# Fused banded attention and two-layer MLP: first loads cut by partitions, two ScalarE copies moved, score blocks ahead of the merged values placed closer together

## The chip, the cores and the metric

One core of one Trainium2 chip. The time is the device time of one launch in microseconds (us); less is better. Engines are called PE (TensorE), DVE (VectorE), ACT (ScalarE), POOL (GpSimd) and SP (SyncE, which here only issues transfers).

## The reference

```python
# q, k, v: (8, 8, 576, 64) fp32; w_in (512, 2048), w_out (2048, 512)
scores = (q @ k.T) / 8
rel = pos[:, None] - pos[None, :]
heads 0-3: keep 0 <= rel < 32             # a band
heads 4-7: keep 0 <= rel < 128, rel % 4 == 0   # a dilated band
attn = softmax(where(keep, scores, -1e9))
x = (attn @ v).transpose(0, 2, 1, 3).reshape(4608, 512)
h = x @ w_in
g = where(h >= 1, h, where(h <= -1, 0, (h + 1)**2 / 4))
out = g @ w_out
```

## The kernel before

**Attention.** Each of the 64 heads is cut into 6 tiles of 96 queries by 128 keys, which hold the whole band. The dilated heads are rearranged on the host so that they have a band too. For each tile: scores (PE), mask and row minimum of the negated scores (DVE, `masked` L360, `lowest` L288), exp with the row sum (ACT, L386), the sum guarded against zero (`guarded`), its inverse (DVE, L418), a product (`normalised`, L423, POOL or DVE), a transpose (on PE for the first 16 heads, `transpose_pe` L470, with the copy out of PSUM `kept` L476; by DVE later, `turned` L434), and the product with v on PE (`weighted` L540, later `values` L628).

**MLP.** 9 blocks of 512 tokens by 16 slices of the 2048 hidden values make 144 steps. One step is 12 matmuls of 512 columns in `layer1` (L670, into a PSUM bank h0 or h1 by the step's parity), the activation, and 12 matmuls in `layer2` two steps later (L726, into acc0 to acc3). Products are made exact enough by splitting fp32 in a high and a low part, three matmuls for each product. The activation of a step is a chain over two engines: `clamped` y (DVE, L680), `squared` (ACT, L683), `activated` (DVE, L686), `g_high` gh (ACT, L693), `g_low` gl (DVE, L697). The last of them is the last reader of the step's PSUM bank.

**Order of the work.** The first 16 heads and the first 18 steps follow a list of tokens written out by hand (`OPENING`), which orders all five engines. In it a letter is an operation and the number a head or step: q, k, Q, K load; S scores, r `lowest`, e exp, T `transpose_pe`, p `kept`, V `weighted`, A `layer1`, B `layer2`, y s j g d the activation chain, and W n are n matmuls on constants that only keep PE busy (`spin` L273). a, b, j, h, l before wi or wo convert the weights, which arrive as 64-bit words; on ACT these are L202, L208 and L220.

From step 18 on, only PE and SP have a written order: `place(u, op)` puts work at a quarter of a half step (three 512-column matmuls). The scheduler puts ACT, DVE and POOL in an order of its own at build time, after what PE's order makes possible. Heads 16 to 63 come in pairs. For one head, `score_block` makes two tiles' scores (L336) at each of three places, and behind the third `after` starts the split of the next head's q and k (ACT `q_high` L242 and `k_high` L245, DVE `q_low` L249, POOL `k_low` L253), loads and `softmax`. Where a pair's first head is a multiple of 4 (from head 20: 11 pairs, called "around" in the code), the three places of its first head stand at 0, 0.75 and 1.5.

Right behind the third of them `values` is called in the middle of an odd step's `layer1`: the products with v of four heads, in three PSUM tiles. The second tile takes the bank h0 of the step before, so its matmuls wait for that step's gl:

```python
plan = (
    ("att", 2, ((n, 0, 5),)),
    (f"h{(s + 1) % 2}", 1, ((n + 2, 4, 6),)),
    ("att", 2, ((n + 2, 0, 4), (n, 5, 6))),
)
```

At six of the 11 places the bank is that of step 6 of a token block (h_6), at five that of step 14 (h_14).

In the opening, q and k of heads 0 and 1 come as one tile of 128 partitions (head 0 on partitions 0 to 63, head 1 on 64 to 127). `load_q` and `load_k` (L146, L162) fetch the columns of the first three query tiles of both heads, `rest_k` and `rest_q` (L136, L133) the other columns. Copies of the transposed probabilities of heads 10 and 11 (tokens p10.1, p11.1) stand on ACT near step 4, between conversions of weights.

Of the kernel before, what the change touches and what calls it, by code (L numbers as in the profile page):

```python
# [30 lines left out]
B, H, S, D = 8, 8, 576, 64  # L31
DM, DF = 512, 2048
WIN, DIL = 32, 4
QT, NQ = 96, 6
KPAD = S + 32
# [7 lines left out]


OPENING = """
q0 k0 msk K0 Q0 q2 k2 q4 mk2 S0.0 S1.0 S0.1 S1.1 k4 S0.2 S1.2 r0.0 wi0 r0.1 e0.0 r0.2 r1.2 e0.1 r1.0 S0.3 r1.1
e0.2 S1.3 S0.4 S1.4 S0.5 e1.1 S1.5 r0.3 e1.2 k8 r0.4 r0.5 e0.3 k6 r1.5 S2.0 S3.0 r1.3 e0.5 S2.1 wi1 r1.4 S3.1
S2.2 e0.4 S3.2 S2.3 q6 S3.3 e1.3 S2.4 r2.0 S3.4 S2.5 i0 S3.5 v0 r2.1 e1.0 R0 r2.5 e1.5 wo0 n0 r2.2 r2.4 e1.4
wo1 r2.3 r3.3 r3.1 v6 r3.0 awi0 r3.2 z2 W6 T0.0 r3.4 e3.3 r3.5 v4 S4.0 i1 S5.0 p0.0 S4.1 e3.4 S5.1 S4.2 S5.2
e3.5 S4.3 R1 S5.3 T0.1 n1 r4.3 e3.0 r4.0 e2 r4.1 r4.2 r5.3 r5.1 e3.2 r5.0 u2 e3.1 W6 S6.0 bwi0 S7.0 S6.1 S7.1  # L50
i3 S6.2 r5.2 S7.2 e4.3 S6.3 R3 S7.3 i2 jwi0 S6.4 e4.2 n3 S7.4 S6.5 S7.5 e4.0 r6.3 r6.0 e4.1 r6.1 e6.3 r6.2
r7.3 W3 S4.4 e6.1 r7.2 r7.1 e6.2 hwi0 r7.0 R2 e6.0 r6.4 S5.4 S4.5 r6.5 S5.5 e6.4 r7.5 T3.0 wi9 r7.4 e6.5 r4.5
# [12 lines left out]
p8.1 hwi4 T9.0 g2 T9.1 B1.0 p9.0 wi15 lwi4 e11 q12 V8.0 p9.1 d2 jwo2 wi12 e10.3 V8.1 e10.2 u11 e10.5 hwo2 B1.1  # L65
wo7 bwi5 y3 i10 B1.2 i11 jwi5 wo14 x8.0.0 lwo2 s3 B1.3 R10 R11 hwi5 j3 A4.0 q14 x8.1.0 x8.1.1 n11 g3 A4.1 n10
wo12 awo3 A4.2 l8.0.0 awi6 A4.3 l8.1.0 bwo3 wo13 l8.1.1 B2.0 d3 bwi6 lwi5 jwo3 B2.1 B2.2 awo4 T11.0 y4 hwo3
T10.0 B2.3 jwi6 p11.0 lwo3 p10.0 s4 A5.0 bwo4 A5.1 j4 hwi6 awi7 T10.1 jwo4 A5.2 g4 p10.1 lwi6 bwi7 A5.3 d4
hwo4 T11.1 V10.0 y5 p11.1 V10.1 jwi7 lwo4 x10.0.0 s5 B3.0 l10.0.0 x10.1.0 j5 x10.1.1 B3.1 hwi7 l10.1.0 awo5
B3.2 lwi7 l10.1.1 awi8 B3.3 bwo5 S12.0 S13.0 g5 S12.1 jwo5 S13.1 S12.2 S13.2 bwi8 S12.3 S13.3 A6.0 d5 hwo5  # L70
r12.0 awo6 r12.1 A6.1 lwo5 r12.2 r12.3 e12.0 r13.3 A6.2 r13.0 bwo6 r13.1 r13.2 A6.3 e13.3 jwi8 e13.2 B4.0 jwo6
hwi8 e13.1 e13.0 y6 S12.4 S13.4 e12.3 S12.5 S13.5 B4.1 r12.4 e12.2 k16 r13.5 s6 r13.4 hwo6 v12 r12.5 B4.2
# [24 lines left out]
def body(ctx, tc, q, k, q2, k2, v, v1, fixed_in, w_in, w_out, out):  # L97
    nc = tc.nc
# [7 lines left out]
    msk = fixed[:QT, : 3 * 128].rearrange("p (k j) -> p k j", k=3)  # L106
# [18 lines left out]
    def borrow(name):  # L125
        return pool.tile([128, 2 * DM], F32, tag=home[name], name=f"{name}_place")

    first_tiles = 3
    first_q, first_k = first_tiles * QT, first_tiles * QT + 32
    whole = {}  # L130

    def rest_q(n):
        nc.sync.dma_start(out=whole["q", n][:, first_q:], in_=q[n // 2][:, first_q:])  # L133

    def rest_k(n):
        nc.sync.dma_start(out=whole["k", n][:, first_k:], in_=k[n // 2][:, first_k:])  # L136

    def load_q(n):
        if f"q{n}" in home:
            qr = borrow(f"q{n}")[:, :S]  # L140
        else:
            tag = "qs" if n < native and n % 4 else "qr"
            qr = pool.tile([128, S], F32, tag=tag, name=f"qr{n}")
        if n < native:
            some = slice(0, first_q if n == 0 else S)
            nc.sync.dma_start(out=qr[:, some], in_=q[n // 2][:, some])  # L146
            whole["q", n] = qr
            for j in range(2):
                heads[n + j]["qs"] = qr[64 * j : 64 * j + 64]
        else:  # L150
            nc.sync.dma_start(out=qr, in_=q2[n - native])
            heads[n]["qr"] = qr

    def load_k(n):
        if f"k{n}" in home:
            kr = borrow(f"k{n}")[:, :KPAD]
        else:
            tag = "kk" if n < native and n % 4 else "kr"
            kr = pool.tile([128, KPAD + 32], F32, tag=tag, name=f"kr{n}")[:, :KPAD]
        if n < native:  # L160
            some = slice(0, first_k if n == 0 else KPAD)
            nc.sync.dma_start(out=kr[:, some], in_=k[n // 2][:, some])  # L162
            whole["k", n] = kr
            for j in range(2):
                heads[n + j]["ks"] = kr[64 * j : 64 * j + 64]
        else:
            nc.sync.dma_start(out=kr, in_=k2[n - native])
            heads[n]["kr"] = kr
# [3 lines left out]
    def load_v(n):  # L172
        width = 2 * NQ * (D + 1 if n in late else D)
        if f"v{n}" in home:
            vt = borrow(f"v{n}")[:, :width]
        else:
            vt = pool.tile([128, width], F32, tag="vt", name=f"vt{n}", bufs=2)
        nc.sync.dma_start(out=vt, in_=v1[n // 2] if n in late else v[n // 2])
        vt = vt.rearrange("p (j t d) -> p j t d", j=2, t=NQ)
        for j in range(2):  # L180
            heads[n + j]["vt"] = vt[:, j]
# [186 lines left out]
    def score_block(n, t0):  # L368
        begin(n)
        scores_split(n, t0)  # L370
        with tc.high_priority(offset=100):
            masked(n, t0)
            lowest(n, t0)
            lowest(n, t0 + 1)
# [64 lines left out]
    def transpose(n):  # L439
        for g in range(3):  # L440
            for half in range(2):
                turned(n, g, half)
# [269 lines left out]
    def layer2(s, m):  # L712
# [31 lines left out]

    operations = {
        "q": load_q, "k": load_k, "v": load_v, "Q": rest_q, "K": rest_k,
        "S": scores, "m": masked, "r": lowest, "z": shifted, "e": exp, "u": summed,
        "i": guarded, "R": inverse, "n": normalised, "T": transpose_pe, "p": kept, "t": turned,
# [21 lines left out]
    def place(u, *ops):  # L770
        slots.setdefault(int(4 * u), []).extend(ops)

    def load(n):
        load_q(n)
        load_k(n)

    def after(m):
        if m < nhead - 1:
            split(m + 1)
        if m < nhead - 2:  # L780
            load(m + 2)
        softmax(m)

    start = 18
    for n in range(native, nhead, 2):
        u = 27 + 4 * (n - native)
        around = n % 4 == 0 and n > native
        for j, ats in enumerate(((0, 0.75, 1.5), (4.5, 5.25, 6)) if around else ((0, 1, 2), (4, 5, 6))):
            for t0, at in zip((0, 2, 4), ats):
                place(u + at, lambda m=n + j, t0=t0: (score_block(m, t0), after(m) if t0 == 4 else None))  # L790
        place(u + (5.5 if around else 4), lambda n=n: (transpose(n), load_v(n)))
        place(u + 8, lambda n=n: transpose(n + 1))
        if n % 4:
            place(u + 10.5, lambda n=n, s=(u + 11) // 2: values(n - 2, s))
# [107 lines left out]
```

## Time and profile before

| | us |
|---|---|
| median of 3 runs | 911.18 (910.76 to 911.56) |
| the profiled execution, its time | 912.0 |
| its span, first to last instruction | 910.2 |
| PE busy | 898.1 (99% of the span) |
| DVE, ACT, POOL busy | 667.8, 489.3, 234.5 |
| mean granted TensorE clock | 0.998 |

The time of an execution is its span and what lies around it, here 1.8 us. The engines' busy times overlap. In the lists of one engine's work below, a row has the start in us, the duration in us, the engine, the line of the kernel, the operation, the tile written and the tile read, the shapes, how many instructions the row joins, and in brackets the idle time just before it with what ended it. Instructions on one engine overlap in part, so that the step from one start to the next is shorter than the duration. The lines of the changed kernel are numbered one lower than those of before from L129 on.

### The profile page before, as it was taken

The numbers are of one execution on the slowest core, as the hardware profiler recorded it, in microseconds if no ns is written. First come the engines' busy times: TensorE is split into PE (matmuls) and PEld (weight loads), VectorE is DVE, ScalarE is ACT, GpSimd is POOL, SyncE is SP. The second block draws the span as 40 slices with busy tenths as digits, with TensorE's granted clock in tenths as the row PEclk, the third lists the DMA queues.
The fourth block names the chain that finished last, engine by engine and source line by source line (L and its number), as shares of the span: only waits on it lengthen the run. The fifth ranks groups of instructions, "written<-read, shape, count | busy, mean of one in ns | idle before, by whom it ended". The sixth has DMA issues, their size and how long they took to land.

```text
span 910.2 us, 14483 instructions
## 1 busy us (share of the span) xinstructions
PE 898.1 (99%) x4855; PEld 739.9 (81%) x4855; DVE 667.8 (73%) x1982; ACT 489.3 (54%) x1402; POOL 234.5 (26%) x163
## 2 busy tenths in 40 slices
PE   8999999999999999999999999999999999999998
PEld 7777887888888888888888888888888888888886
DVE  6897888888888888788888888788888643334333
ACT  7899865545555555555655555555545422223222
POOL 4665571313222212232231322221223000000000
PEclk9999999999999999999999999999999999999999
DMA  8991112212321223222221232222321010001001
GB/s 284 401 381 50 49 37 80 78 59 71 99 90 58 66 64 118 72 71 72 76 84 57 71 104 85 60 70 59 118 71 45 1 47 1 1 0 48 1 1 46
DMA packets 31258, 73.86 MB, mean 81 GB/s; under 512 B 3568, under 2 KB 4432, under 8 KB 31184
## 3 DMA queue, kind: packets, MB, share of 16 engines
q1 hardware_dynamic: 30928, 72.66, 24.4%
q8 instruction: 38, 0.62, 0.3%
q14 instruction: 36, 0.29, 0.1%
q10 hardware_dynamic: 256, 0.28, 0.1%
HBM read 63.49 MB, written 9.44 MB: 80 GB/s over the span
## 4 chain that ended last, share of the span: by engine, by line
PE 69%; DVE 12%; ACT 8%; POOL 6%; issue 3%; DMA 1%; SPq 0%; ACTq 0%; DVEq 0%; POOLq 0%
PE h L670 32%; PE acc L726 32%; POOL kk L253 3%; DVE thirds L434 3%; ACT c L386 2%; PE s L336 2%; POOL c L423 2%; DVE gl L697 2%; PE o L628 2%; DVE pt L434 2%; ACT kk L245 1%; ACT y L683 1%; ACT qs L242 1%; DVE c L360 1%; DVE y L680 1%
## 5 line engine op out<-in xcount | busy, mean ns | idle before, releaser
L726 PE MATMUL acc<-wo,gh 128*128 128x512 f32 x1150 | 383.9, 391 | 0.0
L670 PE MATMUL h<-xh,wi 128*128 128x512 f32 x1152 | 358.7, 393 | 1.4 <-DVE gl L697 1.4
L726 PEld LDWEIGHTS acc<-wo,gh 128*128 128x128 f32 x1150 | 216.1, 188 | 44.0
L670 PEld LDWEIGHTS h<-xh,wi 128*128 128x128 f32 x1152 | 208.0, 188 | 40.8 <-DVE gl L697 1.1
L670 PE MATMUL h<-xl,wi 128*128 128x512 f32 x576 | 224.4, 390 | 0.0
L726 PE MATMUL acc<-wo,gl 128*128 128x512 f32 x575 | 224.1, 390 | 0.0
L386 ACT ACTIVATE c<-c 96x128 f32<-96x128 f32 x330 | 128.3, 393 | 128.0 <-DVE c L288 128.0
L683 ACT ACTIVATE y<-y,consts 128x512 f32<-128x512 f32 x144 | 104.2, 724 | 169.3 <-DVE y L680 168.3
L253 POOL TENSOR_TENSOR kk<-kr,kk 128x608 fp32r<-128x608 f32 x48 | 89.0, 1855 | 408.3 <-ACT kk L245 399.7
L686 DVE TENSOR_TENSOR h<-h,y 128x512 f32<-128x512 f32 x144 | 100.6, 699 | 67.1 <-ACT y L683 66.3
L697 DVE TENSOR_TENSOR gl<-h,gh 128x512 fp32r<-128x512 f32 x144 | 99.0, 687 | 50.6 <-ACT gh L693 49.6
L680 DVE TENSOR_SCALAR y<-h 128x512 f32<-128x512 f32 x144 | 98.4, 683 | 48.2 <-PE h L670 47.8
L693 ACT CAST gh<-h 128x512 fp32r<-128x512 f32 x144 | 84.2, 585 | 91.3 <-PE acc L726 76.1
L670 PEld LDWEIGHTS h<-xl,wi 128*128 128x128 f32 x576 | 108.2, 188 | 23.3
L726 PEld LDWEIGHTS acc<-wo,gl 128*128 128x128 f32 x575 | 108.0, 188 | 20.5 <-DVE gl L697 0.2
L423 POOL TENSOR_TENSOR c<-c 96x768 f32<-96x768 f32 x51 | 74.8, 1466 | 28.5 <-DVE c L418 27.9
L288 DVE CUSTOM_DVE_ANT_0 c<-s,c 96x128 f32<-96x128 f32 x288 | 71.0, 280 | 1.1
L360 DVE TENSOR_TENSOR c<-s,fixed 96x256 f32<-96x256 f32 (+1 forms) x168 | 61.3, 376 | 11.2 <-PE s L336 9.6
L386 ACT ACTIVATION_READ_ACCUMULATOR c<-c 96x1 f32 x318 | 59.7, 188 | 0.0
L434 DVE STREAM_TRANSPOSE thirds<-c 32x192 f32<-32x192 f32 x144 | 53.1, 369 | 8.5 <-POOL c L423 6.9
L336 PEld LDWEIGHTS s<-kk,qs 128*96 128x96 f32 x288 | 46.4, 161 | 15.4
L336 PE MATMUL s<-kk,qs 128*96 128x256 f32 x288 | 57.7, 283 | 0.0
(90 smaller groups left out, 675.4 us busy)
## 6 DMA issues: line engine op xcount, KB each, us to landing
kr<-k_in SPq DMA_DIRECT2D x52, 304.0 KB, 3.2
qr<-q_in SPq DMA_DIRECT2D x52, 288.0 KB, 2.8
vt<-v_in SPq DMA_DIRECT2D x29, 384.0 KB, 3.9
out<-out SPq DMA_DIRECT2D x35, 256.0 KB, 3.2
wi_raw<-w_in SPq DMA_DIRECT2D x16, 512.0 KB, 8.8
wo_raw<-w_in SPq DMA_DIRECT2D x16, 512.0 KB, 9.7
v_place<-v_in SPq DMA_DIRECT2D x3, 384.0 KB, 9.7
k_place<-k_in SPq DMA_DIRECT2D x3, 304.0 KB, 5.4
```

The source lines that it names most:

```text
L253: nc.gpsimd.tensor_tensor(out=kk[:, 1], in0=kr, in1=kk[:, 0].bitcast(F32), op=ALU.subtract)
L336: PE.matmul(out=split_view(n, t0)[:, t - t0], lhsT=hd["qs"][:, t * QT : (t + 1) * QT], rhs=hd["ks"][:, :, t * QT : t * QT + 128], start=Tr ...
L386: nc.scalar.activation(out=c[:, t], in_=c[:, t], func=AF.Exp, bias=st[:, 0, t : t + 1], scale=-1.0, **total)
L423: engine.tensor_tensor(out=c, in0=c, in1=spread(factor(n)), op=ALU.mult)
L434: nc.vector.transpose(out=pt_of(n)[r : r + 32, :, 32 * g : 32 * g + 32], in_=heads[n]["c"][32 * g : 32 * g + 32, :, r : r + 32],)
L670: PE.matmul(out=hps[s], lhsT=ready[f"wi{f}"][:, w, 128 * c : 128 * c + 128], rhs=x[:, c], start=c == 0 and i == 0, stop=c == NC - 1 and i ...
L680: nc.vector.tensor_scalar(out=y, in0=hps[s], scalar1=-1.0, scalar2=1.0, op0=ALU.max, op1=ALU.min)
L683: nc.scalar.activation(out=ys[s], in_=ys[s], func=AF.Square, bias=half_t, scale=0.5)
L686: nc.vector.tensor_tensor(out=hps[s], in0=hps[s], in1=ys.pop(s), op=ALU.max)
L693: nc.scalar.copy(out=gs[s][0], in_=hps[s])
L697: nc.vector.tensor_tensor(out=gl, in0=hps.pop(s), in1=gh.bitcast(F32), op=ALU.subtract)
L726: PE.matmul(out=acc[m], lhsT=g[:, r], rhs=w[:, part], start=f == 0 and i == 0, stop=(f == NF - 1 or s == len(steps) - 2 and m == TOK // 12 ...
```

## The change

It does four things. The first loads of q and k are cut by partitions, not by columns: head 0 whole, then head 1 whole, with Q in front of K, and the scores, minima and exps of these heads follow head by head. The first W6 becomes W3. Two copies on ACT, p10.1 and p11.1, move ahead of g4 and of two weight conversions. The score blocks of the first head of each "around" pair stand at 0, 0.5 and 1.25.

```diff
 OPENING = """
-q0 k0 msk K0 Q0 q2 k2 q4 mk2 S0.0 S1.0 S0.1 S1.1 k4 S0.2 S1.2 r0.0 wi0 r0.1 e0.0 r0.2 r1.2 e0.1 r1.0 S0.3 r1.1
-e0.2 S1.3 S0.4 S1.4 S0.5 e1.1 S1.5 r0.3 e1.2 k8 r0.4 r0.5 e0.3 k6 r1.5 S2.0 S3.0 r1.3 e0.5 S2.1 wi1 r1.4 S3.1
-S2.2 e0.4 S3.2 S2.3 q6 S3.3 e1.3 S2.4 r2.0 S3.4 S2.5 i0 S3.5 v0 r2.1 e1.0 R0 r2.5 e1.5 wo0 n0 r2.2 r2.4 e1.4
-wo1 r2.3 r3.3 r3.1 v6 r3.0 awi0 r3.2 z2 W6 T0.0 r3.4 e3.3 r3.5 v4 S4.0 i1 S5.0 p0.0 S4.1 e3.4 S5.1 S4.2 S5.2
+q0 k0 msk Q0 K0 q2 k2 q4 mk2 S0.0 S0.1 S0.2 S0.3 k4 S0.4 S0.5 r0.0 wi0 r0.1 e0.0 r0.2 r0.3 e0.1 r0.4 S1.0 r0.5
+e0.2 S1.1 S1.2 S1.3 S1.4 e0.3 S1.5 r1.0 e0.4 k8 r1.1 r1.2 e0.5 k6 r1.3 S2.0 S3.0 r1.4 e1.0 S2.1 wi1 r1.5 S3.1
+S2.2 e1.1 S3.2 S2.3 q6 S3.3 e1.2 S2.4 r2.0 S3.4 S2.5 i0 S3.5 v0 r2.1 e1.3 R0 r2.5 e1.4 wo0 n0 r2.2 r2.4 e1.5
+wo1 r2.3 r3.3 r3.1 v6 r3.0 awi0 r3.2 z2 W3 T0.0 r3.4 e3.3 r3.5 v4 S4.0 i1 S5.0 p0.0 S4.1 e3.4 S5.1 S4.2 S5.2
...
-T10.0 B2.3 jwi6 p11.0 lwo3 p10.0 s4 A5.0 bwo4 A5.1 j4 hwi6 awi7 T10.1 jwo4 A5.2 g4 p10.1 lwi6 bwi7 A5.3 d4
-hwo4 T11.1 V10.0 y5 p11.1 V10.1 jwi7 lwo4 x10.0.0 s5 B3.0 l10.0.0 x10.1.0 j5 x10.1.1 B3.1 hwi7 l10.1.0 awo5
+T10.0 B2.3 jwi6 p11.0 lwo3 p10.0 s4 A5.0 bwo4 A5.1 j4 hwi6 awi7 T10.1 jwo4 A5.2 p10.1 g4 lwi6 A5.3 d4 T11.1
+V10.0 y5 p11.1 bwi7 hwo4 V10.1 jwi7 lwo4 x10.0.0 s5 B3.0 l10.0.0 x10.1.0 j5 x10.1.1 B3.1 hwi7 l10.1.0 awo5
...
     def rest_q(n):
-        nc.sync.dma_start(out=whole["q", n][:, first_q:], in_=q[n // 2][:, first_q:])
+        nc.sync.dma_start(out=whole["q", n][64:], in_=q[n // 2][64:])
...
     def load_q(n):
...
-            some = slice(0, first_q if n == 0 else S)
-            nc.sync.dma_start(out=qr[:, some], in_=q[n // 2][:, some])
+            some = slice(0, 64 if n == 0 else 128)
+            nc.sync.dma_start(out=qr[some], in_=q[n // 2][some])
...
     (rest_k and load_k in the same way)
...
-        for j, ats in enumerate(((0, 0.75, 1.5), (4.5, 5.25, 6)) if around else ((0, 1, 2), (4, 5, 6))):
+        for j, ats in enumerate(((0, 0.5, 1.25), (4.5, 5.25, 6)) if around else ((0, 1, 2), (4, 5, 6))):
```

With the last line PE makes a head's second and third block three matmuls earlier, at 11 places. The first two pieces of the order show what that moves on ACT, the third shows the two copies. In the rows, gh is the high part of g, h_14 the bank of step 14, c the probabilities of a head, s_4 its scores of tiles 4 and 5, qs and kk the split q and k of the next head, y the square's tile, pt the transposed probabilities.

ACT ahead of the merged values over bank h_14, before:

```order
L386 ACTIVATE c_2529<-c_2529 96x128 x2
L683 ACTIVATE y_2555<-y_2555,consts 128x512
L386 ACTIVATE c_2529<-c_2529 96x128 x2
L242 CAST qs_2575<-qr_2477 128x576
L245 CAST kk_2576<-kr_2479 128x608
L693 CAST gh_2559<-h_14_2536 128x512
L386 ACTIVATE c_2529<-c_2529 96x128 x2
L412 ACTIVATE c_2529<-c_2529 96x6
```

and in the changed kernel:

```order
L385 ACTIVATE c_2526<-c_2526 96x128 x2
L682 ACTIVATE y_2552<-y_2552,consts 128x512
L241 CAST qs_2569<-qr_2474 128x576
L244 CAST kk_2570<-kr_2476 128x608
L385 ACTIVATE c_2526<-c_2526 96x128 x4
L692 CAST gh_2556<-h_14_2533 128x512
L411 ACTIVATE c_2526<-c_2526 96x6
```

Two exps that followed gh now precede it; the two casts precede the last four exps. On DVE at the same place the two reductions of s_4 (L288) now precede the max L686, which they followed.

ACT ahead of the merged values over bank h_6, before:

```order
L386 ACTIVATE c_2042<-c_2042 96x128 x3
L683 ACTIVATE y_2069<-y_2069,consts 128x512
L386 ACTIVATE c_2042<-c_2042 96x128
L242 CAST qs_2089<-qr_1990 128x576
L245 CAST kk_2090<-kr_1992 128x608
L693 CAST gh_2073<-h_6_2049 128x512
L386 ACTIVATE c_2042<-c_2042 96x128 x2
```

and in the changed kernel:

```order
L385 ACTIVATE c_2039<-c_2039 96x128 x3
L241 CAST qs_2083<-qr_1987 128x576
L682 ACTIVATE y_2066<-y_2066,consts 128x512
L244 CAST kk_2084<-kr_1989 128x608
L385 ACTIVATE c_2039<-c_2039 96x128 x3
L692 CAST gh_2070<-h_6_2046 128x512
```

Here too two more exps stand ahead of gh, and the cast of q has gone ahead of the square.

ACT near step 4 in the opening, before:

```order
L693 CAST gh_942<-h_4_853 128x512
L476 COPY pt_66<-t_4_935 128x192
L208 ACTIVATE wi_raw<-wi_raw 128x512
L220 CAST wo_952<-thirds 128x512
L476 COPY pt_67<-t_4_954 128x192
```

and in the changed kernel:

```order
L475 COPY pt_66<-t_4_932 128x192
L692 CAST gh_940<-h_4_850 128x512
L475 COPY pt_67<-t_4_948 128x192
L207 ACTIVATE wi_raw<-wi_raw 128x512
L219 CAST wo_962<-thirds 128x512
```

Both copies now stand ahead of what they followed: the first ahead of gh, the second ahead of a conversion and a cast of weights. PE's order there is the same.

## Rows read from the trace of the kernel before

**Rows 1.** Part 1 of the page: busy time, share of the span, instructions; and the first line of part 4, the chain that ended last by engine.

```profile
PE 898.1 (99%) x4855; PEld 739.9 (81%) x4855; DVE 667.8 (73%) x1982; ACT 489.3 (54%) x1402; POOL 234.5 (26%) x163
PE 69%; DVE 12%; ACT 8%; POOL 6%; issue 3%; DMA 1%; SPq 0%; ACTq 0%; DVEq 0%; POOLq 0%
```

**Rows 2.** The waits of PE over the whole span: who waited for what, us in total, times, longest.

```profile
PE o L628 <- DVE gl L697: 1.4, 5, 0.3
...
PE o L540 <- ACT pt L476: 1.2, 2, 0.6
```

**Rows 3.** PE in the opening, 6 to 13 us.

```profile
6.68 0.90 PE L321 MATMUL s<-kr,qr 64*96 64x128 f32 x12 [1.23 <-DMA qr<-q_in]
8.20 2.76 PE L321 MATMUL s<-k_place,q_place 64*96 64x128 f32 x24 [0.62 <-DMA k_place<-k_in]
10.89 2.01 PE L273 MATMUL h<-consts 128*128 128x128 f32 x12
12.74 0.49 PE L470 MATMUL t<-fixed,c 96*128 96x96 f32 x4
```

**Rows 4.** Single microseconds of the opening: busy time of each engine, then the granted clock, the mean busy share of the DMA engines, GB/s.

```profile
3.00:4.00 1.00, 1.00 (x6) 0.98 (x5) 0.00 (x0) 0.00 (x0) 0.00 (x0) 1.00 1.05 275
7.00:8.00 1.00, 0.58 (x12) 0.37 (x8) 0.41 (x3) 0.93 (x6) 0.00 (x0) 1.00 1.06 389
```

**Rows 5.** DMA issues of the first 12 us (KB of one, us from issue to landing) for the first columns of k and q, and the chain's piece for k of heads 2 and 3.

```profile
kr<-k_in SPq DMA_DIRECT2D x1, 160.0 KB, 2.9
kr<-k_in SPq DMA_DIRECT2D x1, 144.0 KB, 4.5
...
3.08 4.98 DMA k_place<-k_in
```

**Rows 6.** POOL's product for head 0, which T0.0 reads, and DVE's first reduction of the scores that stand behind T0.0.

```profile
10.90 1.46 POOL L423 TENSOR_TENSOR c<-c 96x768 f32<-96x768 f32 x1 [10.46 <-DVE c L418]
...
14.31 0.29 DVE L288 CUSTOM_DVE_ANT_0 c_place<-s,fixed 96x128 f32<-96x128 f32 x1 [0.39 <-PE s L321]
```

**Rows 7.** ACT near step 4, the two products with v on PE that wait there, and, later, a copy on ACT with the transposes on PE behind it.

```profile
65.57 0.57 ACT L693 CAST gh<-h 128x512 fp32r<-128x512 f32 x1
66.03 0.32 ACT L476 COPY pt<-t 128x192 f32<-128x192 f32 x1
66.25 0.71 ACT L208 ACTIVATE wi_raw<-wi_raw 128x512 uint32<-128x512 uint8 x1
67.34 0.34 ACT L476 COPY pt<-t 128x192 f32<-128x192 f32 x1
...
66.41 0.72 PE L540 MATMUL o<-pt,vt 128*64 128x96 f32 x12 [0.57 <-ACT pt L476]
67.73 0.72 PE L540 MATMUL o<-pt,vt 128*64 128x96 f32 x12 [0.60 <-ACT pt L476]
...
88.21 0.48 ACT L476 COPY pt<-t 128x384 f32<-128x384 f32 x1 [0.25 <-PE t L470]
...
88.73 0.66 PE L470 MATMUL t<-fixed,c 96*128 96x96 f32 x6
```

**Rows 8.** A merged-values place over bank h_14 (524 us): ACT, DVE's gl, and the first two values tiles on PE.

```profile
521.28 0.72 ACT L683 ACTIVATE y<-y,consts 128x512 f32<-128x512 f32 x1 [0.26 <-DVE y L680]
521.91 0.39 ACT L386 ACTIVATE c<-c 96x128 f32<-96x128 f32 x1
...
522.68 0.66 ACT L242 CAST qs<-qr 128x576 fp32r<-128x576 f32 x1
...
523.84 0.57 ACT L693 CAST gh<-h 128x512 fp32r<-128x512 f32 x1
...
524.45 0.69 DVE L697 TENSOR_TENSOR gl<-h,gh 128x512 fp32r<-128x512 f32 x1 [0.32 <-ACT gh L693]
...
524.31 1.05 PE L628 MATMUL o<-pt,vt 128*64 128x96 f32 x20
525.19 1.21 PE L628 MATMUL o<-thirds,vt 128*64 128x96 f32 x24
```

**Rows 9.** A merged-values place over bank h_6 (573 us): the same engines.

```profile
570.48 0.39 ACT L386 ACTIVATE c<-c 96x128 f32<-96x128 f32 x1
...
571.11 0.73 ACT L683 ACTIVATE y<-y,consts 128x512 f32<-128x512 f32 x1 [0.15 <-DVE y L680]
...
573.29 0.57 ACT L693 CAST gh<-h 128x512 fp32r<-128x512 f32 x1
...
573.89 0.69 DVE L697 TENSOR_TENSOR gl<-h,gh 128x512 fp32r<-128x512 f32 x1
...
573.31 1.05 PE L628 MATMUL o<-pt,vt 128*64 128x96 f32 x20
574.64 1.21 PE L628 MATMUL o<-thirds,vt 128*64 128x96 f32 x24 [0.29 <-DVE gl L697]
```

**Rows 10.** DVE's masks (L360) and reductions ahead of that place, and PE's second and third score block, which they read.

```profile
569.73 0.48 DVE L360 TENSOR_TENSOR c<-s,fixed 96x128 f32<-96x128 f32 x2
...
571.14 0.41 DVE L360 TENSOR_TENSOR c<-s,fixed 96x256 f32<-96x256 f32 x1
...
567.95 0.40 PE L336 MATMUL s<-kk,qs 128*96 128x256 f32 x2
...
570.25 0.40 PE L336 MATMUL s<-kk,qs 128*96 128x256 f32 x2
```

More of the change, by code (lines that the diff above doesn't have):

```diff
@@ L128, in body @@
     first_tiles = 3
-    first_q, first_k = first_tiles * QT, first_tiles * QT + 32
     whole = {}
     def rest_q(n):
-        nc.sync.dma_start(out=whole["q", n][:, first_q:], in_=q[n // 2][:, first_q:])
+        nc.sync.dma_start(out=whole["q", n][64:], in_=q[n // 2][64:])
     def rest_k(n):
-        nc.sync.dma_start(out=whole["k", n][:, first_k:], in_=k[n // 2][:, first_k:])
+        nc.sync.dma_start(out=whole["k", n][64:], in_=k[n // 2][64:])
     def load_q(n):
@@ L160, in load_k @@
         if n < native:
-            some = slice(0, first_k if n == 0 else KPAD)
-            nc.sync.dma_start(out=kr[:, some], in_=k[n // 2][:, some])
+            some = slice(0, 64 if n == 0 else 128)
+            nc.sync.dma_start(out=kr[some], in_=k[n // 2][some])
             whole["k", n] = kr
```

## Prediction

> **What bounds the kernel now.** I read the busy times first, then the chain that ended last, then PE's waits, and then the places that the change touches, one engine at a time.
>
> PE is busy 99% of the span, and the chain runs over PE for 69% of it [rows 1]. The matmuls' own number hardly changes (three small ones fewer), so the time can move in only two ways: a wait of PE becomes shorter or longer, or the opening, where the chain runs over transfers, DVE and POOL, becomes shorter or longer. PE's waits are few and small [rows 2, 3]. Three groups of them stand where the change works: the scores of the first heads wait 1.2 us for q and 0.6 us for k of heads 2 and 3, two products with v wait 1.2 us together for copies on ACT, and the merged values wait at five places, 1.4 us together, for a step's gl.
>
> The last one matters most. In a place over bank h_14 [rows 8] the first values tile starts at 524.31 and the second at 525.19, 0.88 later, which is its own length: no wait. But gl, whose bank the second tile takes, starts at 524.45 and lasts 0.69, so it ends at 525.14, 0.05 before the tile starts. There is no slack. In a place over h_6 [rows 9] the two starts are 574.64 - 573.31 = 1.33 apart, so PE already loses 0.45 there. Anything that delays gh, and so gl, delays PE by as much.
>
> **The first loads.** The four transfers keep their 606 KB and their number. S0 needs the first two, S1 all four. PE starts the second half of these scores at 6.68 after a wait for q, and the scores of heads 2 and 3 at 8.20 after a wait for k [rows 3], which lands at 8.06 (3.08 + 4.98) [rows 5]. Head by head or column by column, the same 12 and 12 rows of score matmuls stand before and after the wait, so only the landing counts. The queue moved 275 GB/s in the fourth microsecond with rows of 1152 bytes and 389 GB/s in the eighth with longer ones [rows 4]. If the four loads went at the faster rate, they would take 606/389 = 1.56 us and not 606/275 = 2.20: a gain of 0.65. If a transfer to half of the partitions went at half of the faster rate, they would take 3.11 us: a loss of 0.9. No row shows such a transfer; both ends stay in the range. I take -0.3, half of the gain, since the first load of k alone takes 2.9 us for 160 KB [rows 5], 56 GB/s: most of its time is not set by the rate.
>
> **The spin.** Half of the spin ahead of T0.0 goes. It starts at 10.89 and takes 2.01 [rows 3], so it would end about 1.0 earlier. T0.0 then waits for POOL's product for head 0, which ends at 10.90 + 1.46 = 12.36 [rows 6], against its start now at 12.74: at most 0.3 to 0.4 gained. Behind it stand S4 and S5, and DVE idles 0.39 for the first of them [rows 6] before a run of reductions. So 0.3 can be passed on: -0.3, between -0.4 and 0. The granted clock is not an issue in this sum: PE has work again within half a microsecond.
>
> **The two copies.** V10.0 starts at 66.41 after a wait of 0.57 and V10.1 at 67.73 after 0.60, both for copies on ACT [rows 7]. Now the order there is copy, gh, copy, where before it was gh, copy, conversion, cast, copy. The first copy starts at 65.57 in place of 66.03; a copy takes 0.22 to the next start (66.25 - 66.03) and 0.32 in all, so it ends at 65.90 and V10.0 starts at 65.95. gh follows at 65.79, 0.46 long to the next start; the second copy starts at 66.25 and ends at 66.58. V10.0 is ready for V10.1 at about 66.6, so V10.1 starts at 66.63 in place of 67.73: 1.10 gained. ACT does the same work in all and is busy without a pause there, so what it did first now comes later: some of the gain is lost where PE next waits for ACT. That is at the copy at 88.21 with transposes behind it at 88.73 [rows 7]: ACT waited 0.25 for PE there and its copy ends 0.04 before PE needs it. If ACT can't move, PE keeps only about 0.85. I take -0.85, between -1.1 and 0 (if all is lost again at the next such copy).
>
> **The score blocks, places over h_14.** The order on ACT is fixed at build time: two exps that followed gh now precede it. An exp with its sum takes (522.68 - 521.91)/2 = 0.385 [rows 8]. ACT runs from 521.91 to gh at 523.84 without a pause, so gh starts at 523.84 + 2 x 0.385 = 524.61. gl follows 0.61 behind gh's start and the tile 0.74 behind gl's: 525.96 against 525.19, 0.77 later. Five places: +3.85. Could the blocks' earlier scores bring the chain forward? Each of the four exps is ready when its turn comes, and the square that leads the chain waits for DVE's y, not for a score. So no.
>
> **The score blocks, places over h_6.** Again two exps more precede gh, +0.77. But the cast of q goes ahead of the square and fills ACT's pause there: the exp at 570.48 ends its turn at 570.87, the square starts at 571.11 [rows 9], 0.24. Hence 0.53 later. That is for a place by itself. In the pairs the h_6 place stands 49 us behind an h_14 place where PE has just lost 0.77, and ahead of it DVE is the engine that is late: it masks the second block at 569.73, 1.4 us after PE's 0.40 us of scores at 567.95, and the third at 571.14, half a microsecond after [rows 10]. An engine that is behind PE gets closer when PE stands still, so some of the 0.53 is paid already. I take +0.2 for each of five such places, between 0.1 and 0.53, and +0.5 for the first one, which has no h_14 place ahead: +1.5.
>
> **The sum.** -0.3 - 0.3 - 0.85 + 3.85 + 1.5 = +3.9 on the profiled execution's 912.0: 915.9. That execution was 0.8 above the median of the runs, so I forecast **915.1** as the median. With each term at its own ends this forecast reaches from about 912.8 to 917.5.
>
> **Rivals.**
>
> *The earlier scores help (the other side).* If the blocks' earlier place let DVE and ACT finish a head sooner and gh came free of its queue, the waits at the h_6 places would vanish: five or six of 0.45, some -2.4. With the opening's -1.45 that is 911.2 - 3.85 = 907.3. It is decided by whether the two exps ahead of gh find ACT idle. In the rows ACT has no pause at all between the square and gh over h_14, and 0.15 over h_6; it would need 0.77. Against it. Chance 0.06.
>
> *Nothing is caught up at h_6, and the copies' gain is lost later.* Then each of six h_6 places costs 0.53, 3.2 in place of 1.5, and the opening gives 0.6 and not 1.45: 912.0 + 3.85 + 3.2 - 0.6 = 918.45, less 0.8: 917.6. For it: gl ends just before PE at h_14, so little is spare anywhere. Chance 0.10.
>
> *Half of the partitions load at half the rate.* The opening then loses 0.9 where I take a gain of 0.3: 916.3. For it speaks only that no such transfer has a row; against it, that the second pair goes to the other half and may run beside the first. Chance 0.07. The Trainium skill, SBUF — State Buffer, section "Door 1: The DMA port swizzle", speaks for this rival: partitions 0 to 63 reach only half of the ports that a transfer to all 128 does. It gives 196 GB/s for 64 partitions and 328 for 128 at 1 MiB; by these figures, an estimate, the loads would take 606/196 - 606/328 = 1.2 us longer and the time would be about 916.6. The kernel's trace of before has no load to 64 partitions and can't say.
>
> *The opening gains as said, but only about half of the cost appears at the places*, because DVE's y, which the square waits for at h_14 and h_6 alike, comes earlier once PE lags. Then 911.2 - 1.45 + 2.7 = 912.4: no change that can be measured. Against it: at h_14 ACT's own work alone makes the 0.77, and only 0.26 of idle precedes its square [rows 8]. Chance 0.07.
>
> **How the numbers follow.** The forecast keeps 0.70. A measurement of this kernel can tell 0.2% from no change, 1.8 us: 909.4 to 913.0. Below it lies the first rival (0.06). Within it lie the last one and the lowest end of the forecast: 0.09. Above it lie the others: 0.85. The range from 912.2 to 917.8 takes in the forecast with its ends and the rivals but for the first.
>
> **What would show it.** Right: over h_14, six exps of the head (two, then four with nothing between) ahead of gh, the two values tiles some 1.65 apart in place of 0.88, and PE's waits of L628 for gl at 11 places, 5 us or more in place of 1.4; the two waits for the copies gone; the scores of heads 2 and 3 at about 7.9; T0.0 near 12.1 to 12.4. Wrong: values tiles 0.88 apart over h_14, or gh in the trace ahead of the last exps; the first products with v still waiting; heads 2 and 3 scored at 9 or later. A total under 913 with the values waits as said would mean that the opening holds something that I have missed.

## The result, and the profile after

The changed kernel takes 917.09 us (median of 4 runs, 916.38 to 917.43), the kernel before 911.37 in the same comparison (910.76 to 912.57). The ratio is 1.006, 95% interval 1.0043 to 1.0077: 0.6% slower, inside the range from 912.2 to 917.8, and 2.0 above the forecast of 915.1. The two profiled executions agree: spans of 915.5 and 910.2.

PE's longest waits in the changed kernel (who waits for what: us in total, times, longest) answer to [rows 2]:

```profile
PE o L627 <- DVE gl L696: 4.8, 11, 0.6
...
PE s L320 <- DMA q_place<-q_in: 0.9, 1, 0.9
PE t L469 <- POOL c L422: 0.9, 1, 0.9
PE s L320 <- DMA kr<-k_in: 0.4, 1, 0.4
```

The merged values wait for gl at 11 places and not five, 4.8 us and not 1.4. The two waits of the products with v for ACT's copies are gone. Four waits in the opening are new, the three shown and one of 0.3 for v; those of before for q and for k of heads 2 and 3 are gone.

A place over bank h_14, ACT, DVE and PE, answers to [rows 8]:

```profile
524.40 0.73 ACT L682 ACTIVATE y<-y,consts 128x512 f32<-128x512 f32 x1 [0.27 <-DVE y L679]
525.03 0.66 ACT L241 CAST qs<-qr 128x576 fp32r<-128x576 f32 x1
...
526.20 0.40 ACT L385 ACTIVATE c<-c 96x128 f32<-96x128 f32 x1
...
527.37 0.39 ACT L385 ACTIVATE c<-c 96x128 f32<-96x128 f32 x1
...
527.75 0.56 ACT L692 CAST gh<-h 128x512 fp32r<-128x512 f32 x1
...
528.35 0.69 DVE L696 TENSOR_TENSOR gl<-h,gh 128x512 fp32r<-128x512 f32 x1 [1.34 <-ACT gh L692]
...
527.48 1.05 PE L627 MATMUL o<-pt,vt 128*64 128x96 f32 x20
529.09 1.21 PE L627 MATMUL o<-thirds,vt 128*64 128x96 f32 x24 [0.56 <-DVE gl L696]
```

The pause in front of the square is 0.27 (before 0.26). From the square's start to gh's it is now 3.35 us (before 523.84 - 521.28 = 2.56), and the second values tile starts 1.61 behind the first (before 0.88). DVE stands idle for 1.34 waiting for gh: it is ACT's queue that is late.

A place over bank h_6 answers to [rows 9, 10]:

```profile
573.15 0.28 DVE L287 CUSTOM_DVE_ANT_0 c<-s,c 96x128 f32<-96x128 f32 x1
...
575.06 0.72 ACT L682 ACTIVATE y<-y,consts 128x512 f32<-128x512 f32 x1
...
577.45 0.56 ACT L692 CAST gh<-h 128x512 fp32r<-128x512 f32 x1
...
573.21 0.39 PE L725 MATMUL acc<-wo,gh 128*128 128x512 f32 x1
573.59 0.45 PE L335 MATMUL s<-kk,qs 128*96 128x256 f32 x2
...
577.43 1.05 PE L627 MATMUL o<-pt,vt 128*64 128x96 f32 x20
578.78 0.96 PE L627 MATMUL o<-thirds,vt 128*64 128x96 f32 x17 [0.31 <-DVE gl L696]
```

Here the two values tiles start 1.35 apart, as before (1.33). The new loss is earlier: the third score block starts 0.38 behind the matmul in front of it, where a matmul takes 0.23 to the next start. It needs the PSUM bank of the first block (two banks serve the blocks in turn), which DVE's reduction at 573.15 still reads.

Step by step, the starts of layer 1 in the two traces differ by this much (changed less before):

| at the start of | before, us | changed, us | difference |
|---|---|---|---|
| the first layer 1 | 27.36 | 27.77 | +0.41 |
| step 6, behind the two copies | 72.39 | 71.66 | -0.73 |
| step 9 | 92.08 | 91.69 | -0.39 |
| the end (spans) | 910.2 | 915.5 | +5.3 |

### The profile page after: what moved, and what is told of

It reads as the page before. It is cut to its first block, busy times and chain, and to the rows that moved or that the text cites. A ratio compares the mean times of both kernels' runs of the same rounds, so it can differ in the third digit from the quotient of the medians.

```text
span 915.5 us, 14471 instructions
## 1 busy us (share of the span) xinstructions
PE 900.8 (98%) x4849; PEld 740.1 (81%) x4849; DVE 668.6 (73%) x1982; ACT 491.0 (54%) x1402; POOL 236.1 (26%) x163
## 4 chain that ended last, share of the span: by engine, by line
PE 63%; DVE 13%; ACT 10%; POOL 8%; issue 4%; DMA 2%; SPq 0%; ACTq 0%; DVEq 0%; POOLq 0%
PE h L669 29%; PE acc L725 29%; ACT c L385 4%; POOL kk L252 3%; DVE thirds L433 3%; POOL c L422 3%; PE s L335 2%; DVE gl L696 2%; DVE pt L433 2%; ACT y L682 2%; PE o L627 2%; ACT kk L244 1%; ACT qs L241 1%; PE s L320 1%; DVE c L359 1%
```

## The experiments

The theory after the result: the slots cost 5.6 through ACT's order and the early third block, the copies give back 0.8 as forecast, and the opening loses about 1 us against its forecast. The first batch takes the slots and the loads apart, the second and third look for what the opening loses.

**Which score block.**

```diff
-((0, 0.5, 1.25), (4.5, 5.25, 6))
+((0, 0.5, 1.5), (4.5, 5.25, 6))
```

> The changed kernel, but only the second score block moved (0, 0.5, 1.5). Theory (ACT's order): the third block's place decides what stands ahead of gh; with it back, two exps follow gh again, the values tiles over h_14 stand 0.88 apart and not 1.61, the wait at the third block over h_6 goes, and the time is 917.1 - 5.3 = about 911.8. Rival (blocks closer together crowd DVE, whichever moves): about half comes back, 914.5, with the tiles over h_14 some 1.2 apart.

Measured: 911.48 (10 runs; ratio to before 1.0003, 0.9994 to 1.0012). PE in a place over h_14:

```profile
523.67 1.05 PE L627 MATMUL o<-pt,vt 128*64 128x96 f32 x20
524.55 1.21 PE L627 MATMUL o<-thirds,vt 128*64 128x96 f32 x24
```

0.88 apart. In the trace the difference to the kernel before hardly moves between step 9 (-0.47) and step 64 (-0.59). Moving the second block alone costs nothing.

```diff
-((0, 0.5, 1.25), (4.5, 5.25, 6))
+((0, 0.75, 1.25), (4.5, 5.25, 6))
```

> The changed kernel, but only the third score block moved (0, 0.75, 1.25). Theory (ACT's order): all of the cost stays, values tiles over h_14 1.61 apart, 917.1. Rival (crowding): about 914.5, tiles over h_14 some 1.2 apart.

Measured: 917.36 (4 runs; 1.0072, 1.0055 to 1.0089), with the tiles over h_14 again 1.60 to 1.63 apart. All of the cost that can be told hangs on the third block's place, behind which the scheduler puts the casts and exps. Crowding, the rival, falls.

**Hiding the wait instead of removing it.**

```diff
-            place(u + 10.5, lambda n=n, s=(u + 11) // 2: values(n - 2, s))
+            place(u + 10.75, lambda n=n, s=(u + 11) // 2: values(n - 2, s))
```

> The changed kernel with the merged values placed three matmuls (0.68 us) later on PE; order on ACT unchanged. Theory (PE loses only what it waits for gl): the waits in the changed kernel are 0.73 at five places and 0.50 at six, 6.6 together; 0.68 more matmuls ahead hide all but 0.05 at five: 917.1 - 6.4 = 910.7, and the waits of L627 for gl go from 4.8 us to under 0.5. Rival (the wait moves on: the copies out of the second tile's bank end later and the next step's layer 1 waits for that bank): half comes back, 914, with new waits of L669 for xl or xh.

Measured: 911.74 (10 runs; 1.0005, 0.9996 to 1.0014). The order on ACT stays, and gl is late as in the changed kernel, yet PE no longer waits for it:

```profile
524.70 0.56 ACT L692 CAST gh<-h 128x512 fp32r<-128x512 f32 x1
...
525.29 0.69 DVE L696 TENSOR_TENSOR gl<-h,gh 128x512 fp32r<-128x512 f32 x1 [1.34 <-ACT gh L692]
...
525.12 1.05 PE L627 MATMUL o<-pt,vt 128*64 128x96 f32 x20
526.03 1.21 PE L627 MATMUL o<-thirds,vt 128*64 128x96 f32 x24
```

0.91 apart and no wait of L627 for gl in the list of waits. Over the kernel before, +5.7 became +0.7: 5.1 of the expected 6.4 came back. What stayed is the early third block's wait (0.2 at each h_6 place) and some 0.2 in the layer 1 behind each h_14 place. Most of the cost of the slots is the wait for gl in front of the second values tile.

**The loads and the scores of heads 0 and 1.** The edit restores the order of the first four lines but for W3, with alternating scores (`S0.0 S1.0 S0.1 S1.1 ...`), and the column cut of the loads, and leaves W3, the copies and the slots as changed.

> The changed kernel with the first four loads cut by columns again and the scores of heads 0 and 1 alternating again, with the short spin, the copies and the slots as changed. Theory (scoring head by head ends late and holds the SP queue's load k8 back, so q6 comes late): k8 is issued at 7.6 and not 9.5, the scores of head 6 don't wait for q6, the first layer 1 starts at 27.1 to 27.3 in place of 27.77, and the time is 916.4. Rival (the short spin loses it): the first layer 1 stays at 27.7 and the time at 917.1.

Measured: 916.02 (4 runs; 1.0056, 1.0041 to 1.0071), and in its trace the first layer 1 starts at 26.35. By the trace this is 1.4 earlier than in the changed kernel, by the medians 0.8 to 1.3 less (+4.9 over before, against +5.7 of the changed kernel and +6.3 of the run with the third block, which has the same opening). The intervals overlap; the direction is that of the trace. The opening's loss lies in the loads and scores, not in the short spin. The scores of head 6 still wait 0.65 for q6, which the expectation had ruled out. PE there, the 24 rows of heads 0 and 1 and the 24 of heads 2 and 3:

```profile
4.20 0.90 PE L321 MATMUL s<-kr,qr 64*96 64x128 f32 x12
6.23 0.90 PE L321 MATMUL s<-kr,qr 64*96 64x128 f32 x12 [1.13 <-DMA qr<-q_in]
8.05 1.55 PE L321 MATMUL s<-k_place,q_place 64*96 64x128 f32 x24 [0.92 <-DMA k_place<-k_in]
```

In the changed kernel, PE and then SP's issues:

```profile
4.71 4.12 PE L320 MATMUL s<-kr,qr 64*96 64x128 f32 x21 [0.43 <-DMA kr<-k_in]
...
10.90 0.93 PE L272 MATMUL h<-consts 128*128 128x128 f32 x6
12.72 0.55 PE L469 MATMUL t<-fixed,c 96*128 96x96 f32 x4 [0.89 <-POOL c L422]
...
16.91 0.35 PE L320 MATMUL s<-k_place,q_place 64*96 64x128 f32 x2 [0.91 <-DMA q_place<-q_in]
```

```profile
1.36 0.58 SPq L161 DMA_DIRECT2D kr<-k_in  x1
1.99 0.59 SPq L132 DMA_DIRECT2D qr<-q_in  x1
...
9.49 0.33 SPq L161 DMA_DIRECT2D kr<-k_in  x1
...
10.82 0.44 SPq L145 DMA_DIRECT2D q_place<-q_in  x1
```

Twenty-one rows of one head at a time take 4.1 us, where twelve of alternating heads take 0.9. The load behind them (at 9.49) waits for their buffer, and q6 stands behind that load. Two candidates follow: SP's queue, and PE's pace.

**SP's queue.**

```diff
-... e0.4 k8 r1.1 ... S2.3 q6 S3.3 ...
+... e0.4 r1.1 ... S2.3 q6 k8 S3.3 ...
```

> The changed kernel with k8, SP's load into the buffer that the scores of heads 0 and 1 hold until 9.3, moved behind q6 on SP. Theory (the late end of these scores costs time through SP's queue): k6, wi1 and q6 are issued before 9 us, q6 lands before 16, the wait of 0.9 us for it in front of the scores of head 6 goes, the first layer 1 starts up to 0.9 earlier than 27.77, 916.2 to 916.6. Rival (DVE is behind there anyway): the first layer 1 stays at 27.7 and the time at 917.1.

Measured: 917.22 (4 runs; 1.0065, 1.005 to 1.008). q6 is issued at 7.21, the wait in front of head 6 goes:

```profile
16.10 1.85 PE L320 MATMUL s<-k_place,q_place 64*96 64x128 f32 x24
```

and the first layer 1 still starts at 27.59. My theory fell: the wait for q6 is real and costs at most 0.2; in its place PE now waits 0.6 in all for DVE a little later.

**PE's pace.**

```diff
-                spin(7, scored[n, t0])
+                spin(8, scored[n, t0])
```

> The changed kernel with 8 in place of 7 spin matmuls ahead of the first scores, which fills the 0.43 us that PE waits for k0. Theory (that pause keeps PE at the low level): rows of score matmuls 0.107 us apart from about 5 us on, head 1's scores end near 7.9 and not 9.3, k8 is issued near 8.0, 916.2. Rival (the scores of one head alone keep it there, pause or not): rows 0.21 us apart until heads 2 and 3 as now, 917.1.

Measured: 916.54 (4 runs, 915.48 to 917.33; 1.0057, 1.0042 to 1.0072). In the trace, heads 0 and 1 and then heads 2 and 3:

```profile
5.04 2.97 PE L320 MATMUL s<-kr,qr 64*96 64x128 f32 x24 [0.34 <-DMA kr<-k_in]
8.33 1.55 PE L320 MATMUL s<-k_place,q_place 64*96 64x128 f32 x24 [0.32 <-DMA k_place<-k_in]
```

The scores start 0.33 later and end earlier, and the first layer 1 starts at 26.48 in place of 27.77. By the medians it is +5.7 over before, like the changed kernel, and 0.7 less than the run with k8 late beside it. Its four runs lie apart, 915.48 and 916.04 (the one traced) and 917.04 and 917.33, so the trace may speak for two of them only.

```diff
-                spin(7, scored[n, t0])
+                spin(10, scored[n, t0])
```

> The changed kernel with 10 in place of 7 spin matmuls ahead of the first scores: PE works without a pause until about 5.1, past the landing of k0. Theory (the pause ahead of the first scores keeps PE at its low level): rows of the first scores 0.107 us apart, heads 2 and 3 scored by 9.7, the first layer 1 near 26.5 as with 8 spins, 916.1 to 916.5 in spite of the later start. Rival (the one look with 8 spins was luck, the level varies by itself): rows 0.21 apart again, first layer 1 near 28, 917.2 or more.

Measured: 916.20 (5 runs; 1.0056, 1.0042 to 1.0069), +4.9 over before. But for the first three, the rows of heads 0 and 1 come at the fast pace again, 24 in 2.79 us from 5.48 on. The first layer 1 starts at 27.23, not at 26.5: k of heads 2 and 3 landed later in this execution, and PE waited for it:

```profile
9.10 1.55 PE L320 MATMUL s<-k_place,q_place 64*96 64x128 f32 x24 [0.82 <-DMA k_place<-k_in]
```

The same longer spin in the kernel before:

> The kernel before with 10 in place of 7 spin matmuls ahead of its first scores. Theory (the level decides about 1 us of the opening, and in some executions of this kernel it is low too): first scores start near 5.1 in place of 4.2, but 0.107 apart and done before q comes; heads 2 and 3 scored by 9.7, first layer 1 near 26.4 in place of 27.36, 910.3. Rival (the level in this stretch decides nothing): 910.9 to 911.1, first layer 1 at 27.3.

Measured: 911.89 (11 runs; 1.0006, 0.9997 to 1.0015). A miss: the pace is fast, heads 2 and 3 are done by 10.3 and not 9.7, the first layer 1 starts at 27.41. Here the longer spin ends some 1.2 us after the first load has come (4.17), PE later waits 1.03 for q6, and nothing is gained.

**Order alone, with the loads of before.**

```diff
-S0.0 S1.0 S0.1 S1.1 k4 S0.2 S1.2 ... S1.3 S0.4 S1.4 S0.5 e1.1 S1.5
+S0.0 S0.1 S0.2 S1.0 k4 S1.1 S1.2 ... S0.4 S0.5 S1.3 S1.4 e1.1 S1.5
```

> The kernel before with its loads, but the scores of heads 0 and 1 one head after the other within each half. Theory (two heads run beside each other on the two halves of PE's rows, and one after the other they take twice as long): the first 12 rows take about 1.9 in place of 1.24 and the last 12 about 1.3 to 2.6 in place of 0.9, the last scores end near 8.0 to 9.2 in place of 7.5, and k8 is issued as much later; 911.3 to 911.9. Rival (order makes no difference, only the loads do): the last scores end at 7.5, 911.1.

Measured: 910.96 (10 runs; 1.0005, 0.9996 to 1.0015). No cost that can be told; the 0.5 to 1.1 expected did not come, and the first layer 1 starts at 26.32. One head after the other takes longer (24 rows without a break in 2.92 us), but they ended at 7.3, no later than in the kernel before, because PE used the time in which it otherwise waits for q. So the order by heads alone, with the full pace from 6 us on, is not the loss.

**The short spin alone** (`W6` to `W3` in the kernel before).

> The kernel before with the spin ahead of T0.0 halved and nothing else. As forecast: T0.0 waits for POOL's product and gains 0.3, 910.6. Rival (POOL's product decides, the spin was hidden): no change, 910.9.

Measured: 911.45 (11 runs; 0.9999, 0.9991 to 1.0008). POOL's product, and PE's transposes behind it:

```profile
10.29 1.47 POOL L423 TENSOR_TENSOR c<-c 96x768 f32<-96x768 f32 x1 [9.85 <-DVE c L418]
...
11.81 0.55 PE L470 MATMUL t<-fixed,c 96*128 96x96 f32 x4 [1.05 <-POOL c L423]
```

The spin ended early and PE waited for POOL, as the rival has it. The interval, 0.8 us to either side, can't tell a gain of 0.3 from none. With the full spin PE waits for POOL at this place in two other traces (0.81 in the run with the order alone, 0.38 in the kernel before with 10 spins): there the spin was hidden.

**The copies alone** (the two last lines of the list, in the kernel before).

> The kernel before with the two copies moved and nothing else. As forecast: the two waits of V10.0 and V10.1 (1.2 us) go, 1.1 gained at step 6 and 0.8 kept from step 9 on, 910.1. Rival (ACT gives all of it back later): 910.9.

Measured: 910.68 (12 runs; 0.9996, 0.9987 to 1.0004): by time alone unclear, 0.6 less than before. The trace shows it: against the trace of before the difference goes from -0.61 at the first layer 1 to -1.71 at step 6 and -1.42 at step 9, a gain of 1.10 of which 0.81 stays.

**A version that beats both**: the kernel before with the short spin, the two copies and the merged values three matmuls later.

> The kernel before with the short spin and the two copies as changed, and the merged values 0.68 us later; loads, scores and slots of before. Theory (three of the parts gain and add up): the copies 0.8, the spin 0.1 to 0.3, the waits for gl 2.4 less 0.9 for waits that move behind the values as seen in the run with the values later: 911.1 - 2.5 = 908.6, at most 909.2. Rival (the waits only move on): 910.2.

Measured: 908.38 (5 runs; 0.9966, 0.9953 to 0.9979), against 910.81 of before: 2.4 faster. In all 12 merged-values places the first two tiles start 0.88 apart, and the wait of L628 for gl is gone from the list. In its trace the difference to before goes from -0.99 at step 20 to -3.36 at the last step, so 2.4 of the gain lies where the values stand; the copies and the spin were not taken out of this version one by one.

## Why the prediction was right, and where it was off

**Places over h_14: right.** Two exps more ahead of gh were to cost 0.77 at each of five. The tiles start 0.73 further apart at each [rows 8], 3.65 in all.

**Places over h_6: the size right, the way only in part.** I took +0.5 for the first and +0.2 for the others. At the first the tiles' distance grew from 1.05 to 1.38, 0.33, and at the second from 1.22 to 1.38; at the other four it stayed (1.33 to 1.38 before, 1.35 to 1.41 now). gh's delay was absorbed there, as the argument from [rows 10] had it. The 0.2 is another wait: the third score block now comes before DVE has released its PSUM bank. The row was at hand: DVE's masks of the second block start 1.4 behind PE's scores [rows 10]. I used this lateness only as a reason for catching up, not as a bank that would still be held. The slots in all: forecast +5.35, measured about +5.6.

**The copies: right.** V10.0 and V10.1 now run without a break, and ACT's later copy has moved only 0.37:

```profile
65.96 0.31 ACT L475 COPY pt<-t 128x192 f32<-128x192 f32 x1
...
66.32 1.42 PE L539 MATMUL o<-pt,vt 128*64 128x96 f32 x24
...
87.84 0.47 ACT L475 COPY pt<-t 128x384 f32<-128x384 f32 x1
...
88.01 0.74 PE L469 MATMUL t<-fixed,c 96*128 96x96 f32 x6
```

From +0.41 to -0.73 is 1.14 gained, and 0.34 is given back by step 9: 0.07 at the transposes behind the copy that I had named [rows 7], and 0.27 at the product with v behind them. 0.80 is kept against 0.85.

**The short spin: wrong by 0.3.** T0.0 started at 12.72 in the changed kernel, at 12.74 before. POOL's product became the bound, as I had it [rows 6], but it did not stay at 12.36: it moves with the scores in front of it, and in the changed kernel it ends at 12.67.

```profile
11.20 1.47 POOL L422 TENSOR_TENSOR c<-c 96x768 f32<-96x768 f32 x1 [10.75 <-ACT c L385]
```

**The loads: the step that failed.** It reads: "the same 12 and 12 rows of score matmuls stand before and after the wait, so only the landing counts." The landing came as forecast in this trace: k of heads 2 and 3 lands at 7.75, 0.3 earlier. That was luck in part: over seven traces of each cut it lands between 7.51 and 8.65 (columns) and between 7.70 and 8.96 (partitions). The rival of half the rate fell: the last of the four loads lands at 6.49 and not at 6.55, and over the same traces at 6.20 to 6.49 where the cut by columns gave 5.98 to 7.14. By the figures of the Trainium skill's "Door 1: The DMA port swizzle" (SBUF — State Buffer), an estimate, the loads would have taken some 1.2 us longer; these traces don't show that for four loads of which two go to either half.

What counted was the pace, together with the order by heads. SP's first five issues take 0.57 to 0.60 where they took 0.39 to 0.45 (the fifth load is cut in neither kernel, so the cut alone does not explain it); k of head 0 comes at 4.57 and not at 4.08, and PE pauses 0.43 between the spin and the first scores. Behind that pause the score rows came at half the pace, 0.21 us from start to start where one head stands alone, until all rows of heads 0 and 1 were done near 9 us, in each of the five traces with these loads and seven spin matmuls; with one or three matmuls more ahead of them, soon at the full pace, 0.11. In all 14 traces the pace is half until the trace's records of the granted clock set in, with 1.00, and full from the next few rows on; ahead of that moment there is no record:

| kernel | pause ahead of the first scores | first clock record | heads 0 and 1 scored, last row starts | first layer 1 |
|---|---|---|---|---|
| before | none listed | 4.95 (0.50 from 8.37 to 11.78) | 7.31 | 27.36 |
| loads back (alternating heads) | none listed | 4.23 | 6.86 | 26.35 |
| before, order alone by heads | none listed | 6.06 | 7.01 | 26.32 |
| before with the copies alone | none listed | 10.37 | 7.35 | 26.75 |
| the version that beats both | none listed | 10.56 | 7.64 | 27.11 |
| changed, and four with its loads and 7 spins | 0.32 to 0.52 | 9.73 to 12.62 | 8.84 to 9.05 | 27.59 to 28.20 |
| changed, 8 spins | 0.34 | 5.20 | 7.74 | 26.48 |
| changed, 10 spins | none listed | 6.11 | 8.00 | 27.23 |

So neither half of the step does it by itself. The order by heads with the full pace from 6.06 or 5.20 on cost nothing (26.32, 26.48), and alternating heads at half the pace still start their last row at 7.35 and 7.64, since two rows run beside each other. One head at a time at half the pace, from 4.7 on, is what ends near 9. With the copies alone:

```profile
4.23 1.60 PE L321 MATMUL s<-kr,qr 64*96 64x128 f32 x12
6.17 1.60 PE L321 MATMUL s<-kr,qr 64*96 64x128 f32 x12 [0.34 <-DMA qr<-q_in]
7.71 2.83 PE L321 MATMUL s<-k_place,q_place 64*96 64x128 f32 x24
```

The opening was to gain 0.6 ahead of the first layer 1 and lost 0.41. That is 1.0 of the 2.0 by which the forecast missed; 0.25 lies in the slots, and 0.65 in the step from trace to median: I took off 0.8, and the changed kernel's profiled execution was only 0.15 above its median. The 0.41 itself is measured against a trace of before whose clock fell back; the table shows how much the opening varies between single executions of the same loads. By the medians the loads cost 0.8 to 1.3 where I had -0.3. That the pause is what keeps the pace low is not shown: it goes with the low pace in five of five traces, but 8 spins leave a pause of 0.34 at the full pace, and two traces without a listed pause have the low pace past 10 us. What sets the moment of the first clock record stays open. Why POOL's and DVE's chain behind it turns 1.5 us of scoring into about 1 us at layer 1 was not taken apart.

**The range.** The terms at their own ends add up to 913.9 and 919.1, not to 912.8 and 917.5 as the prediction says. The measured time lies inside either pair, and 0.7 below the upper end of the range from 912.2 to 917.8.

**The rivals.** That earlier scores help fell at the places named. That only half of the slots' cost appears (912.4) fell too: 3.65 of 3.85 came over h_14 alone. Nothing caught up at h_6 (917.6) was close in time by accident: at four of the six h_6 places the tiles did not move apart, and the copies' gain was kept.

## What to carry to other kernels

Moving work earlier on one engine can hand another engine an order in which its urgent instruction comes last; read the new order of the engine that feeds the next wait, count what now stands ahead of the urgent one, and check what still holds the buffer that the earlier work needs. If the consumer can be put a little later at no cost, that hides the delay without touching the late engine: three matmuls moved in front of the values hid every wait of the values for gl, and with the old slots, the copies and the short spin this beat both kernels.

## What the runs showed of the hardware that was not expected

Score matmuls of two heads that use the two halves of PE's rows run beside each other: alternating, 24 rows take 1.55 us; one head at a time, 24 rows take 2.8 to 3.0 at the fast pace.

The granted clock in the table of windows does not tell the pace in the first microseconds. The rows of the kernel before at 9 us and of the changed kernel at 5 us:

```profile
9.00:10.00 1.00, 1.00 (x13) 1.00 (x12) 0.00 (x0) 1.00 (x7) 0.00 (x0) 0.50 1.05 409
...
5.00:6.00 1.00, 1.00 (x6) 1.00 (x6) 0.00 (x0) 0.00 (x0) 0.00 (x0) 1.00 0.90 282
```

In the first the column says 0.50 (1.2 GHz), and the 24 rows of heads 2 and 3 take 2.76 [rows 3] against 1.55 at a granted 1.00 (2.4 GHz). In the second it says 1.00, yet the six rows of one head start 0.21 us apart, against 0.11 behind 8 spins. The reason is in the records: the changed kernel's trace has no record of the clock ahead of 9.73, and the column counts a stretch without a record as 1.00. That PE is at its lower level there is inferred, not recorded: the 24 rows of heads 2 and 3 take 2.83 and 2.76 ahead of the first record in two traces (the copies alone, the version that beats both), as in the stretch of before that is recorded as 0.50.
